# Loading Q, K and V in more, smaller DMAs: five opening loads and all loads of the regular groups are split in two

## The chip, the cores and the metric

The kernel runs on one core of one Trainium2 chip. The metric is device time in microseconds (us) of one execution, as the median of several runs. Engines are named as in the profile: PE is TensorE (PEld its weight loads), DVE is VectorE, ACT is ScalarE, POOL is GpSimd, SP is SyncE, which only issues DMAs here. A "q" behind a name (SPq) is the engine's sequencer.

## What is computed

A retention layer (attention with a decay in place of the softmax) feeds a bilinear feed-forward layer. Q, K and V are float32 of 8 batches x 8 heads x 576 positions x 64.

```python
scores = scale * np.matmul(q, k.transpose(0, 1, 3, 2))
gamma = 1.0 - 2.0 ** (-5.0 - np.arange(H))
Dmat = np.where(rel >= 0, gamma[:, None, None] ** rel, 0.0)
attn = np.matmul(scores * Dmat, v)              # rel = query position - key position
x = attn.transpose(0, 2, 1, 3).reshape(4608, 512)
out = ((x @ w_a) * (x @ w_b)) @ w_out           # 512 -> 1536 -> 512
```

## The kernel before

**Stages.** The 4608 rows of x are made in groups of 256 rows and taken by the feed-forward layer in blocks of 512, 256, 256 and then 512 rows. The feed-forward matmuls (lines 771, 794 and 809 for the two first products, 828 for the last) run through the whole kernel; the retention work of later groups is put between them at places written out by hand.

- *Opening and third batch, by steps.* The first 256 rows of batches 0, 1 and 2 are handled in six steps, `STEPS`, each a batch and four of its heads. `load_step` (line 155) loads four heads of Q, K or V of one step: partition p holds rows 2p and 2p + 1 of each head, so a run in memory is 512 bytes and a load is 256 KB. Twelve such loads (steps 0 to 3) open the kernel in an order written out by hand: step 0's Q, K, V; step 2's Q, K; step 1's K, Q; step 2's V; step 3's K, Q; step 1's V; step 3's V. All are issued by SP but step 0's K, which ACT issues. Steps 4 and 5 are loaded later in the same way.
- *Regular groups.* Groups 3 to 17 hold 256 rows each of all eight heads. `load_pair` (line 139) loads Q, K and V of one; each tensor in two DMAs, one for each 128 rows (all heads, runs of 256 bytes, 256 KB). Two of the groups (15 and 17) hold the last 64 rows of eight batches and are loaded in four DMAs of 64 rows (128 KB) for each tensor; they are called left-over groups.

**What uses the loads.** Of a step, `cast_step` (line 311) turns Q and K to bfloat16 on DVE, ACT or POOL, `values_step` (319 and 321) scales V by the decay, the transposes (329) run on PE and are copied by ACT or DVE (333), and the scores, states and outputs follow on PE. ACT also makes tables (213, 223) and copies states (386 to 391). Of a regular group, `ahead` casts Q and K on POOL, the first 64 partitions in one instruction (484) and the other 64 in two (488), and scales V (495); for groups 4 and 5 K and V are cast one half (128 rows) at a time. `turn` (507) then issues from SP two DMA transposes of the casts. `keyed` (538), `matched` (600), `from_states` (628) and `keys_into` (641) are the group's matmuls.

**Order.** Every engine works through its instructions in the order of the program. SP's order is: the opening loads; a tiny DMA `gate` (line 930) that waits for the first third of `w_out`; the loads of steps 4 and 5; group 3; group 4's Q; then in turn the transposes of one group, the loads of a later group, and stores of finished rows (lines 750 and 752). Places of this order are numbers in a list, `todo`, along the feed-forward work. Weights are loaded by POOL's own DMA queue (lines 264, 266 and 269), the first of them behind POOL's casts of the opening.

Of the kernel before, what the change touches and what calls it, by code (L numbers as in the profile page):

```python
# [18 lines left out]
def kernel(  # L19
# [10 lines left out]
    nc = tc.nc  # L30

    B, H, S, D = q.shape
    DM = H * D
# [30 lines left out]
    def rows_of(n):  # L64

        if n not in LEFT:
            b, m = PAIRS[n]
            return [(kp, 0, 128, b, 256 * m + 128 * kp) for kp in (0, 1)]
        return [(i // 2, 64 * (i % 2), 64, 4 * LEFT[n] + i, S - 64)
                for i in range(4)]  # L70
# [67 lines left out]
    paired = {}  # L138

    def load_pair(n, which=(0, 1, 2)):  # L140
        if n >= NP:
            return
        paired.setdefault(n, {})
        for i in which:
            name, src = (("qf", q), ("kf", k), ("vf", v))[i]
            t = stage.tile([128, 2 * DM], FP32, tag=name, name=name + "2")
            for kp, r0, m, b, s0 in rows_of(n):
                nc.sync.dma_start(
                    t[r0:r0 + m, kp * DM:(kp + 1) * DM]
                    .rearrange("p (h d) -> p h d", h=H),  # L150
                    src[b, :, s0:s0 + m, :].rearrange("h s d -> s h d"))
            paired[n][i] = t

    def load_step(n, hh, which, on=nc.sync):

        if n not in paired:
            paired[n] = [stage.tile([128, 2 * DM], FP32, tag=name, name=name)
                         for name in ("qf", "kf", "vf")]
        on.dma_start(  # L159
            paired[n][which][:, hh * DM:(hh + 1) * DM]  # L160
            .rearrange("p (h e) -> p h e", h=4),
            (q, k, v)[which][n, 4 * hh:4 * hh + 4, 0:256, :]
            .rearrange("h (p two) d -> p h (two d)", two=2))

    STEPS = [(0, 0), (1, 0), (0, 1), (1, 1), (2, 0), (2, 1)]
    Q, K, V = 0, 1, 2
    for i, which in ((0, Q), (0, K), (0, V), (2, Q), (2, K), (1, K),
                     (1, Q), (2, V), (3, K), (3, Q), (1, V), (3, V)):
        load_step(*STEPS[i], which,
                  nc.scalar if (i, which) == (0, K) else nc.sync)  # L170

# [327 lines left out]
    def turn(n):  # L501
        qkb = of(natural, n)[0]
        qkT = qkt_pool.tile([128, 2, 2, HP, 128], BF16, tag="qkT",
                            name="qkT2")
        transposed[FIRST + n, "pair"] = qkT
        for w in (Q, K):
            nc.sync.dma_start_transpose(
                qkT[:, w].rearrange("p k c s -> p (k c) s"), qkb[:, w])
        if n > 10:
            load_pair(n + 2)  # L510
# [420 lines left out]
    for i, which in ((4, Q), (4, K), (4, V), (5, Q), (5, K), (5, V)):  # L931
        load_step(*STEPS[i], which)
    load_pair(FIRST)
    load_pair(FIRST + 1, (Q,))


# [131 lines left out]
```

## Time and profile before

| | us |
|---|---|
| median of 3 runs (324.93 to 325.23) | 325.18 |
| the profiled execution | 325.43 |
| its span (first to last instruction) | 323.7 |

DMAs by kind in that execution, with the median time from issue to landing:

| DMA | number, size | us to landing |
|---|---|---|
| Q, SP | 32 of 256 KB, 8 of 128 KB | 4.7, 3.2 |
| K, SP | 31 of 256 KB, 8 of 128 KB | 4.8, 3.5 |
| V, SP | 32 of 256 KB, 8 of 128 KB | 5.2, 4.2 |
| K of step 0, ACT | 1 of 256 KB | 4.0 |
| transposes, SP | 30 | 3.7 |

"Issue" is the time that an instruction takes on the issuing engine, waits included; "to landing" counts from the start of the issue until the last part of the data has been reported as written. In a line of the timeline the columns are start and length in us, engine, line, operation, tile, shape, number of instructions and, in brackets, how long the engine had been idle and what ended it.

### The profile page before, as it was taken

The page shows a single profiled execution, that of the slowest core. Times are in us where ns is not written, and L with a number is a line of the kernel's source. Part 1 is how long each engine was busy: PE and PEld are TensorE (multiplying, and loading weights), DVE is VectorE, ACT ScalarE, POOL GpSimd, SP SyncE. Part 2 cuts the span into 40 slices and gives each one's busy share as a digit, 9 for nine tenths or more (in the row PEclk, how much of TensorE's full clock was granted, in tenths as well). Part 3 has the DMA queues.
Part 4 walks back from the last instruction along what each step waited for, and adds up shares of the span by engine and source line. Part 5 has one row for each costly group of instructions (what it writes and reads, how often), then busy time and mean ns, then how long its engine had stood idle before and what let it go on. Part 6 is the DMA issues. An engine that isn't in the chain of part 4 may idle for free.

```text
span 323.7 us, 8631 instructions
## 1 busy us (share of the span) xinstructions
PE 314.0 (97%) x3573; PEld 164.4 (51%) x3611; DVE 165.4 (51%) x294; ACT 131.5 (41%) x293; POOL 118.8 (37%) x158
## 2 busy tenths in 40 slices
PE   7899999999999999999999999999999999999996
PEld 3564457778444554444454545454445444444444
DVE  5744445665546754835374626562566256514321
ACT  7735753463435523533253324442433343313321
POOL 4990077574755274447165305450530000000000
PEclk9999999999999999999999999999999999999999
DMA  8999999999999999999999169935840520031013
GB/s 216 255 196 207 259 231 189 200 176 206 174 221 223 195 208 206 269 222 263 175 197 216 52 163 198 207 74 144 194 86 19 104 76 2 2 97 32 1 23 108
DMA packets 145431, 50.90 MB, mean 157 GB/s; under 512 B 126704, under 2 KB 140912, under 8 KB 145392
## 3 DMA queue, kind: packets, MB, share of 16 engines
q1 hardware_dynamic: 140112, 45.37, 68.4%
q0 software_dynamic: 4752, 4.72, 8.8%
q8 instruction: 28, 0.46, 0.6%
q10 hardware_dynamic: 528, 0.26, 0.3%
q14 instruction: 11, 0.09, 0.1%
HBM read 37.75 MB, written 9.44 MB: 146 GB/s over the span
## 4 chain that ended last, share of the span: by engine, by line
PE 92%; DMA 2%; SPq 2%; ACT 1%; issue 1%; DVE 1%; DVEq 0%
PE pb L809 29%; PE po L828 29%; PE pa L794 28%; DMA qf<-in_q_dram 2%; SPq L159 2%; PE sc L600 1%; PE o L628 1%; PE o L641 1%; PE kv L538 1%; PE pa L771 1%; ACT state_after L386 0%; ACT vb L319 0%; PE tp L329 0%; DVE hT L814 0%; ACT own L390 0%
## 5 line engine op out<-in xcount | busy, mean ns | idle before, releaser
L814 DVE TENSOR_TENSOR hT<-ha,pb 128x512 bf16<-128x512 bf16 (+1 forms) x120 | 75.9, 633 | 94.8 <-PE pb L809 86.6
L802 ACT CAST ha<-pa 128x512 bf16<-128x512 f32 (+1 forms) x120 | 64.8, 543 | 115.9 <-PE pa L794 109.9
L809 PE MATMUL pb<-xT,wb_sb 128*128 128x512 bf16 (+1 forms) x474 | 111.2, 357 | 0.5
L794 PE MATMUL pa<-xT,wa_sb 128*128 128x512 bf16 (+1 forms) x452 | 106.9, 356 | 1.2 <-issue 0.6
L828 PE MATMUL po<-wo_sb,hT 128*128 128x512 bf16 (+2 forms) x442 | 94.7, 367 | 1.7 <-issue 1.4
L809 PEld LDWEIGHTS <-wb_sb 128*128 128x128 bf16 x480 | 47.0, 98 | 46.6 <-issue 0.3
L794 PEld LDWEIGHTS <-wa_sb 128*128 128x128 bf16 x468 | 45.0, 98 | 44.4 <-issue 0.2
L828 PEld LDWEIGHTS <-hT 128*128 128x128 bf16 x456 | 42.7, 98 | 47.2
L484 POOL CAST qkb<-qf 64x1024 bf16<-64x1024 f32 x15 | 15.5, 1031 | 64.4 <-DMA qf<-in_q_dram 55.1
L495 POOL TENSOR_TENSOR vb<-vf,vs 128x1024 bf16<-128x1024 f32 (+1 forms) x17 | 28.9, 1700 | 13.3 <-DMA vf<-in_v_dram 6.1
L839 DVE COPY osb<-po 128x512 f32<-128x512 f32 (+2 forms) x17 | 11.1, 653 | 43.0 <-PE po L828 43.0
L837 ACT COPY osb<-po 128x512 f32<-128x512 f32 (+1 forms) x21 | 12.0, 573 | 43.4 <-PE po L828 40.5
L484 POOL CAST qkb<-kf 64x1024 bf16<-64x1024 f32 (+1 forms) x17 | 16.4, 966 | 16.7 <-DMA kf<-in_k_dram 16.5
L563 DVE TENSOR_TENSOR sums<-kv,sums 128x256 f32<-128x256 f32 x44 | 18.7, 424 | 2.8 <-PE kv L538 0.8
L609 DVE TENSOR_TENSOR sT<-sc,mask 128x512 bf16<-128x512 f32 x30 | 19.4, 681 | 0.0
L488 POOL CAST qkb<-kf 64x512 bf16<-64x512 f32 (+1 forms) x34 | 18.7, 579 | 1.0
L488 POOL CAST qkb<-qf 64x512 bf16<-64x512 f32 x30 | 17.6, 615 | 0.6
L567 ACT CAST states<-sums 64x512 bf16<-64x512 f32 x26 | 16.0, 617 | 0.3
L654 DVE TENSOR_TENSOR xT<-o,qs 128x512 bf16<-128x512 f32 x24 | 15.4, 682 | 1.5 <-PE o L641 1.5
L311 POOL CAST qkb<-kf 128x512 bf16<-128x512 f32 x5 | 3.1, 617 | 16.9 <-DMA kf<-in_k_dram 16.9
L355 DVE TENSOR_TENSOR sT<-sc,mask_s 128x1024 bf16<-128x1024 f32 x6 | 7.2, 1222 | 1.3 <-PE sc L347 1.2
L855 PE MATMUL w<-ones 128*128 128x512 bf16 x17 | 6.3, 482 | 1.5 <-DVE idxp_f L204 1.5
(88 smaller groups left out, 163.5 us busy)
## 6 DMA issues: line engine op xcount, KB each, us to landing
qf<-in_q_dram SPq DMA_DIRECT2D x32, 256.0 KB, 4.7
vf<-in_v_dram SPq DMA_DIRECT2D x32, 256.0 KB, 5.2
kf<-in_k_dram SPq DMA_DIRECT2D x31, 256.0 KB, 4.8
out_dram<-osb SPq DMA_DIRECT2D x25, 256.0 KB, 3.2
out_dram<-osb SPq DMA_DIRECT2D x21, 128.0 KB, 2.6
wo_sb<-in_moe_w_out_dram POOLq DMA_DIRECT2D x3, 512.0 KB, 16.7
qf<-in_q_dram SPq DMA_DIRECT2D x8, 128.0 KB, 3.2
kf<-in_k_dram SPq DMA_DIRECT2D x8, 128.0 KB, 3.5
```

What stands on the lines that cost most here:

```text
L484: nc.gpsimd.tensor_copy(qkb[0:64, w, e], t[0:64, e])
L488: nc.gpsimd.tensor_copy(to[:, :, 1 - r], fro[:, :, r])
L495: nc.gpsimd.tensor_tensor(vb[:, e].rearrange("p (h d) -> p h d", d=D), t[:, e].rearrange("p (h d) -> p h d", d=D), decay[:, at], op=ALU.mult)
L563: nc.vector.tensor_tensor(sums[:, i], own, prev, op=ALU.add)
L567: nc.scalar.copy(to(half(1 - r)), fro(half(r)))
L609: nc.vector.tensor_tensor(sT[:, on].rearrange("p c k s -> p (c k) s"), sc[:, on].rearrange("p c k s -> p (c k) s"), mask3.unsqueeze(1).to_ ...
L654: nc.vector.tensor_tensor(x_of(t0, 128).rearrange("p c (a s) -> p c a s", a=2), o[:, :, :, kp].rearrange("p a c s -> p c a s"), qs[:, :, s ...
L794: nc.tensor.matmul(pa[:, 0:n], wa_sb[:, c, fs], xT[:, c], start=(c == 0), stop=(c == NC - 1))
L802: nc.scalar.copy(ha[:, 0:n], pa[:, 0:n])
L809: nc.tensor.matmul(pb[:, 0:n], wb_sb[:, c, fs], xT[:, c], start=(c == 0), stop=(c == NC - 1))
L814: nc.vector.tensor_tensor(hT[:, F, 0:n], has[F][:, 0:n], pb[:, 0:n], op=ALU.mult)
L828: nc.tensor.matmul(po[:, 0:width], hT[:, F, u * 128:(u + 1) * 128], wo_sb[:, F, cols], start=(F == 0), stop=(F == NF - 1))
```

## The change

In `load_pair`, a DMA for 128 rows becomes two: heads 0 to 3, then heads 4 to 7 (128 KB each). The 64-row DMAs of the left-over groups stay whole. In `load_step` a new argument `parts` says into how many DMAs of equal numbers of heads a load goes; the opening list gives 2 to five loads (step 2's Q and K, step 1's Q, step 3's K, step 1's V) and 1 to the seven others. The loads of steps 4 and 5 use the default, 1. The order of the loads, the bytes, the tiles and all instructions that read them stay.

```diff
-                nc.sync.dma_start(
-                    t[r0:r0 + m, kp * DM:(kp + 1) * DM]
-                    .rearrange("p (h d) -> p h d", h=H),
-                    src[b, :, s0:s0 + m, :].rearrange("h s d -> s h d"))
+                heads = H if m < 128 else H // 2
+                for h in range(0, H, heads):
+                    e0 = kp * DM + h * D
+                    nc.sync.dma_start(
+                        t[r0:r0 + m, e0:e0 + heads * D]
+                        .rearrange("p (h d) -> p h d", h=heads),
+                        src[b, h:h + heads, s0:s0 + m, :]
+                        .rearrange("h s d -> s h d"))
...
-    def load_step(n, hh, which, on=nc.sync):
+    def load_step(n, hh, which, on=nc.sync, parts=1):
...
-        on.dma_start(
-            paired[n][which][:, hh * DM:(hh + 1) * DM]
-            .rearrange("p (h e) -> p h e", h=4),
-            (q, k, v)[which][n, 4 * hh:4 * hh + 4, 0:256, :]
-            .rearrange("h (p two) d -> p h (two d)", two=2))
+        for h in range(0, 4, 4 // parts):
+            hs = slice(4 * hh + h, 4 * hh + h + 4 // parts)
+            on.dma_start(
+                paired[n][which][:, 128 * hs.start:128 * hs.stop]
+                .rearrange("p (h e) -> p h e", h=4 // parts),
+                (q, k, v)[which][n, hs, 0:256, :]
+                .rearrange("h (p two) d -> p h (two d)", two=2))
...
-    for i, which in ((0, Q), (0, K), (0, V), (2, Q), (2, K), (1, K),
-                     (1, Q), (2, V), (3, K), (3, Q), (1, V), (3, V)):
+    for i, which, parts in ((0, Q, 1), (0, K, 1), (0, V, 1), (2, Q, 2),
+                            (2, K, 2), (1, K, 1), (1, Q, 2), (2, V, 1),
+                            (3, K, 2), (3, Q, 1), (1, V, 2), (3, V, 1)):
```

More of the change, by code (lines that the diff above doesn't have):

```diff
@@ L158, in load_step @@
                          for name in ("qf", "kf", "vf")]
-        on.dma_start(
-            paired[n][which][:, hh * DM:(hh + 1) * DM]
-            .rearrange("p (h e) -> p h e", h=4),
-            (q, k, v)[which][n, 4 * hh:4 * hh + 4, 0:256, :]
-            .rearrange("h (p two) d -> p h (two d)", two=2))
+        for h in range(0, 4, 4 // parts):
[5 more added lines that the diff above has]
+                .rearrange("h (p two) d -> p h (two d)", two=2))
     STEPS = [(0, 0), (1, 0), (0, 1), (1, 1), (2, 0), (2, 1)]
     Q, K, V = 0, 1, 2
-    for i, which in ((0, Q), (0, K), (0, V), (2, Q), (2, K), (1, K),
-                     (1, Q), (2, V), (3, K), (3, Q), (1, V), (3, V)):
+    for i, which, parts in ((0, Q, 1), (0, K, 1), (0, V, 1), (2, Q, 2),
+                            (2, K, 2), (1, K, 1), (1, Q, 2), (2, V, 1),
+                            (3, K, 2), (3, Q, 1), (1, V, 2), (3, V, 1)):
         load_step(*STEPS[i], which,
-                  nc.scalar if (i, which) == (0, K) else nc.sync)
+                  nc.scalar if (i, which) == (0, K) else nc.sync, parts)
     idxp_i = const.tile([128, 2], INT32)
```

## The prediction

> **What bounds the kernel now.** I read the page's shares first, then the chain of work that ended last.
>
> ```profile
> span 323.7 us, 8631 instructions
> PE 314.0 (97%) x3573; PEld 164.4 (51%) x3611; DVE 165.4 (51%) x294; ACT 131.5 (41%) x293; POOL 118.8 (37%) x158
> ...
> PE 92%; DMA 2%; SPq 2%; ACT 1%; issue 1%; DVE 1%; DVEq 0%
> ```
>
> TensorE (PE) is busy for 314.0 of 323.7 us and is 92% of the chain. The rest, DMA, SP's issues and ScalarE (ACT), lies at the start. The second view is that chain in order of time, from 4 to 17 us (start, length, what).
>
> ```profile
> 6.56 5.51 DMA qf<-in_q_dram
> 12.07 0.02 issue
> 12.09 0.62 ACT qkb L311
> ...
> 14.09 0.95 ACT vb L319 x4
> ...
> 16.64 0.18 ACT second L391
> 16.82 0.27 PE pa L771
> ```
>
> A Q load lands at 12.07 (step 3's, the tenth opening load), ACT casts it and is then busy link after link until 16.82, when the first feed-forward product may start. From 16.82 on the chain is TensorE to the end; the idle times that the groups show before its matmuls (0.5, 1.2 and 1.7 us for the three feed-forward lines) are over the whole run. So loads can be worth something in two ways only: a gain before 16.82, or a loss where TensorE comes to wait for a later load. The third view is the timeline of the opening, for the slack of that chain.
>
> ```profile
> 11.27 0.60 ACT L223 ACTIVATE qs_o<-qs_o,biasq,lgp 128x256 f32<-128x256 f32 x1
> 12.09 0.62 ACT L311 CAST qkb<-qf 128x512 bf16<-128x512 f32 x1 [0.22 <-DMA qf<-in_q_dram]
> ...
> 16.80 2.52 PEld L771 LDWEIGHTS <-wa_sb 128*128 128x128 bf16 x24 [0.17 <-DMA wa_sb<-in_moe_w_a_dram]
> ```
>
> ACT stood idle for 0.22 us before that cast. An earlier Q therefore gives 0.22 us at most, unless ACT's earlier work moves too; a later Q costs its whole delay.
>
> **The change, part by part.** It adds DMAs and removes none of the bytes. Five opening loads become ten DMAs. Thirteen regular groups (15 groups less the two of left-over rows) have three loads of two DMAs each, so 78 DMAs become 156. Together 83 more issues, all on SP.
>
> *Price of a half's issue.* No row shows a regular half (4 heads x 128 rows x 256 B). The nearest are the whole opening loads, 4 heads x 128 rows with runs of 512 B, at 0.45 to 0.51 us while SP is not held up, and the left-over loads, also 128 KB in runs of 256 B, but 8 heads x 64 rows, at 0.63 us. A whole regular load takes 0.57 to 0.63 us after a pause and 1.14 us when SP runs ahead of the transfers. I take 0.51 plus 0.04 between issues, 0.55 us, because the heads and rows are the same; the other end is 0.67. SP's timeline:
>
> ```profile
> 53.34 1.27 SPq L148 DMA_DIRECT2D kf<-in_k_dram  x2
> 54.72 1.90 SPq L148 DMA_DIRECT2D vf<-in_v_dram  x2
> 56.79 4.56 SPq L507 DMA_TRANSPOSE qkT<-qkb  x2
> ...
> 64.74 3.77 SPq L148 DMA_DIRECT2D vf<-in_v_dram  x2
> ...
> 190.56 2.78 SPq L148 DMA_DIRECT2D qf<-in_q_dram  x4
> ```
>
> Where SP runs ahead, two halves (1.10 us) cost no more than one whole (1.14 + 0.04), so groups 3 and 5 to 14 keep their pace: 78 x 0.55 = 43 us more of issuing is covered by SP's waiting for the transfers. If a half costs 0.67, twelve halves take 8.0 us where group 5's six wholes took 7.05 (61.45 to 68.50): 1.0 us late at its end.
>
> *Where that cover is thin.* Group 4's K and V are issued at 53.34 onto a nearly drained queue, so wholes are cheap there: 53.34 to 56.62, against 8 x 0.55 = 4.4, to 57.7. Behind them on SP stand the transposes of group 4, which wait for the casts on POOL (GpSimd), and behind those group 5's loads.
>
> ```profile
> 56.99 0.61 POOL L484 CAST qkb<-kf 64x512 bf16<-64x512 f32 x1 [1.10 <-DMA kf<-in_k_dram]
> ...
> 58.45 0.61 POOL L484 CAST qkb<-kf 64x512 bf16<-64x512 f32 x1
> ...
> 59.94 1.04 POOL L495 TENSOR_TENSOR vb<-vf,vs 128x512 bf16<-128x512 f32 x1
> ...
> 64.31 0.45 PE L600 MATMUL sc<-qkT 64*64 64x64 bf16 x32
> ```
>
> The first cast wants all 8 heads of the first 128 rows, which now come with the second half, issued at 53.89. At 3.1 us to landing (smallest of the left-over loads) it is there at 56.99, as before; at the 3.6 us of the whole it is 0.55 late. The K transpose was issued at 59.88 and took 3.7 us: landed at 63.6, 0.7 us ahead of the matmul at 64.31. I take 0.1 us late, since two halves hold the bytes of one whole and the queue is nearly empty; it is hidden. The same slack is 1.6 us at group 3 (52.0 + 3.6 against 57.16), 1.9 at group 5 (71.9 + 3.1 against 76.93) and more than 2 at the later groups. Middle: 0, bounds 0 and +0.65 (below, as a rival). A gain is excluded, because TensorE waits for no load there.
>
> *More landings to wait for.* A consumer of a split tile waits for two to four landings. Such semaphore waits show as 17 ns on SP; 15 POOL instructions in the tight stretch would add some 0.2 us at most, inside the 0.7.
>
> *The opening.* SP's first loads (step 0's Q and V) are unchanged, K is on ACT. Then come Q2 and K2 in halves, K1, Q1 in halves, V2, K3 in halves, Q3, V1 in halves, V3. At 0.55 each Q3 would be issued at 0.80 + 11 x 0.55 = 6.9, against 6.56. The trace's records give the DMAs eight completion semaphores in turn, and a DMA waits for the landing of the one eight places before it: Q3 then waits for K2's first half, shortly before 7.57 (K2's landing, 2.40 + 5.2), and goes at about 7.3. Before, it took 5.5 us from issue to landing in a queue that was never empty: the transfers are behind, not SP. About 4.7 us of time are left to 12.07 and the left-over loads need 3.1 to 4.5, so Q3 lands where the queue brings it. Value 0. Bounds: -0.22 (the idle time of ACT) and +0.1 from the semaphore waits.
>
> The rate of the transfers gives the reason for the lower bound (stretch, its length, busy times of PE, PEld, DVE, ACT, POOL, clock, DMA share, GB/s):
>
> ```profile
> 3.00:4.50 1.50, 1.50 (x5) 0.45 (x3) 0.36 (x2) 1.45 (x7) 0.07 (x1) 1.00 1.15 343
> 5.00:12.00 7.00, 5.90 (x130) 3.54 (x133) 4.97 (x9) 5.19 (x14) 4.28 (x7) 1.00 1.17 290
> 61.50:64.50 3.00, 2.95 (x100) 1.82 (x101) 1.80 (x4) 1.90 (x5) 1.04 (x1) 1.00 1.15 256
> 65.00:68.00 3.00, 2.84 (x19) 1.37 (x15) 2.83 (x7) 1.90 (x4) 1.65 (x3) 1.00 1.23 220
> ```
>
> Each time the rate is higher before SP's issues stretch and lower once they are stretched. If halves keep SP from running ahead, the fast rate may last.
>
> A rule speaks against the change: "DMA: Bandwidth & Descriptors" of the Trainium skill, Rules for kernel authors, wants many small transfers joined into large ones, and its Anatomy of one DMA gives a fixed cost of about 2.0 us each (for the software path). Paid one after another, 83 of them would be 166 us, and the estimate 491 us. The trace disagrees with paying them in series: loads take 4.0 to 5.6 us to land and yet leave SP every 0.5 to 1.1 us.
>
> **Sum.** 0 + 0. The profiled execution took 325.43 us (span 323.7 and 1.7 around it), 0.25 over the median of 325.18; so about 325.2 us.
>
> **Rivals.**
> *The weights get in front of V (slower).* The first weight load leaves POOL at 9.07 and lands 7.7 us later; step 3's V was issued at 8.53 and lands 5.4 later, at 13.9, and ACT's scaling by it is on the chain at 14.09. With halves V goes out at about 9.1, level with the weights. From the moment that it falls behind them it waits for their transfer: 384 KB at some 200 GB/s, 2.0 us, less the 0.16 of slack: up to +1.8, 327.0; when they mix, half of it, 326.1. For it: the tiny gate DMA needed 5.2 us behind weights. Against it: V's issue still begins no later. The same page (Queues, rings and completion order) says that the engines take turns between queues packet by packet; by that V would be delayed in part, while the gate's 5.2 us looks more like first come, first served, which spares V.
>
> *Group 4 is late (slower).* With issues every 0.67 us the sixth half (V's first rows) goes at 56.69 and lands 4.6 later (as V did there), at 61.3, 1.35 us after POOL wanted it at 59.94; less 0.7 of slack, TensorE waits 0.65 us: 325.8. The point is a delay of 0.7. For it: the smallest slack of all. Against it: the halves need less time to land.
>
> *The fast rate lasts (faster).* 7.5 us at 290 GB/s would be 6.3 at 343: Q3 1.17 us earlier. ACT takes 0.22 of it, 325.0, within no change; if its work before moves as well, all of it, 324.0. Against: a V load of step 0, which is not split, feeds ACT first, and TensorE's order sits between.
>
> **How the numbers follow.** A measurement of this kernel can tell about 0.2%, 0.65 us. No change, 0.45 with the small gain in it. Weights in front of V, 0.2; group 4 or a slower transfer of halves in other groups, 0.18: together slower 0.38. Faster 0.17. The likeliest gives 325.2. Its own range is 324.9 to 325.8; the rivals stretch it to 324.2 and 326.9.
>
> **What would show it.** Right: Q3's landing still near 12.1, the first feed-forward product at 16.6 to 16.9, the matmul of group 4 at 64.3 with no wait, SP's halves at about 0.55 us. Wrong: the rate after 5 us near 343, V after 14.1, or TensorE waiting at a line of the groups (538, 600, 628).

## The result, and the profile after

| | before | after |
|---|---|---|
| median of the runs taken side by side (22 each), us | 325.19 | 326.27 |
| lowest and highest, us | 324.90, 327.49 | 325.31, 328.41 |
| after / before (95%) | | 1.0032 (1.0019 to 1.0045) |
| the profiled execution, us | 325.43 | 325.31 |
| its span, us | 323.7 | 323.6 |

The change makes the kernel 0.32% slower, 1.1 us. The executions of the new kernel also spread more: 6 of its 22 lie between 325.3 and 325.7, the 16 others from 326.05 upwards. Of the kernel before, 20 of 22 lie below 326. The profiled execution of the new kernel is its quickest, so its page can show where the change makes the kernel tighter, but hardly the loss. The slowest, 328.41, is no measure of the change: it ran at a mean granted clock of 0.995 in place of 1.000, and so did one execution of the kernel before beside a later run (327.94; more in the last section). All line numbers are 7 higher than before.

The page of the new kernel, head, first line of part 1 and the chain that ended last:

```profile
span 323.6 us, 8794 instructions
...
PE 317.5 (98%) x3611; PEld 164.1 (51%) x3611; DVE 165.6 (51%) x294; ACT 131.3 (41%) x293; POOL 117.9 (36%) x158
...
PE 94%; DMA 3%; POOL 1%; DVE 1%; issue 0%; SPq 0%; DVEq 0%; POOLq 0%
```

TensorE is the whole bound, as before. (3573 matmuls were recorded before and 3611 now, the same number as weight loads: 38 records were missing then.) The opening, by ACT's timeline and by the windows that the prediction used:

```profile
12.15 0.62 ACT L318 CAST qkb<-qf 128x512 bf16<-128x512 f32 x1 [0.20 <-DMA qf<-in_q_dram]
...
14.03 1.07 ACT L326 ACTIVATE vb<-vf,vs 128x64 bf16<-128x64 f32 x4
```

```profile
3.00:4.50 1.50, 1.50 (x5) 0.45 (x3) 0.33 (x2) 1.44 (x7) 0.06 (x1) 1.00 1.15 342
5.00:12.00 7.00, 6.28 (x132) 3.48 (x133) 4.92 (x9) 5.21 (x14) 4.21 (x7) 1.00 1.18 290
61.50:64.50 3.00, 3.00 (x132) 1.85 (x131) 1.70 (x5) 1.62 (x4) 1.51 (x2) 1.00 0.94 194
65.00:68.00 3.00, 3.00 (x16) 1.35 (x15) 2.93 (x7) 2.19 (x4) 0.03 (x1) 1.00 0.80 178
```

Step 3's Q is there at 12.13 (before 12.07) and the idle time in front of its cast is 0.20 (before 0.22). The rate after 5 us is 290 GB/s in both kernels. In the same two stretches of the regular groups it fell, from 256 and 220 GB/s to 194 and 178, and the DMA engines are no longer always busy: 128 KB every 0.55 us are 238 GB/s at most, and SP begins group 5's loads later. SP's timeline shows it, first at groups 4 and 5:

```profile
53.38 2.21 SPq L151 DMA_DIRECT2D kf<-in_k_dram  x4
55.70 2.09 SPq L151 DMA_DIRECT2D vf<-in_v_dram  x4
57.97 4.03 SPq L514 DMA_TRANSPOSE qkT<-qkb  x2
62.10 2.21 SPq L151 DMA_DIRECT2D qf<-in_q_dram  x4
64.35 3.15 SPq L151 DMA_DIRECT2D kf<-in_k_dram  x4
67.60 2.10 SPq L151 DMA_DIRECT2D vf<-in_v_dram  x4
70.24 4.15 SPq L514 DMA_TRANSPOSE qkT<-qkb  x2
```

Four halves take 2.1 to 2.2 us, 0.55 each, as costed, but for those of 3.15, of which one alone took 1.49 us. Group 4's K and V were issued from 53.34 to 56.62 before and to 57.79 now. Group 4's transposes therefore begin at 57.97 in place of 56.79 and group 5's loads at 62.10 in place of 61.45. Their issuing ends at 69.70 in place of 68.50. The lateness is handed on: the transposes of groups 3 to 12 all begin 1.2 to 3.7 us later than before, and only those of group 13, ahead of which SP has time to spare in both kernels, begin on time again. Group 11's transposes before and after:

```profile
154.08 3.67 SPq L507 DMA_TRANSPOSE qkT<-qkb  x2
```

```profile
157.01 2.85 SPq L514 DMA_TRANSPOSE qkT<-qkb  x2
```

SP begins them 2.9 us later, and K's, the second of the two, 1.9 later. The product that wants them, on TensorE's timeline before and after:

```profile
162.94 0.50 PE L600 MATMUL sc<-qkT 64*64 64x64 bf16 x32
```

```profile
162.59 0.50 PE L607 MATMUL sc<-qkT 64*64 64x64 bf16 x32
```

Their K lands at 162.33, 0.26 us ahead of it; before it landed at 159.66, 3.3 us ahead. So this execution has no wait, but its margins are nearly used up. Worked out from the landings in the trace, this is the time from the landing of a group's K transpose to its product `sc` (line 600 before, 607 after), in us:

| group | 3 | 4 | 5 | 6 | 8 | 9 | 10 | 11 | 13 | 14 |
|---|---|---|---|---|---|---|---|---|---|---|
| before | 1.6 | 0.7 | 1.9 | 6.8 | 6.5 | 4.8 | 5.9 | 3.3 | 4.3 | 7.4 |
| after | 1.7 | 0.1 | 0.4 | 5.8 | 3.7 | 2.0 | 2.1 | 0.3 | 4.3 | 7.5 |

In this execution, a landing that comes half a microsecond later would make TensorE wait at group 4, 5 or 11, and would have cost nothing before.

Not all of this is SP's doing. The products themselves come 0.3 us earlier than before, because the opening ended 0.3 earlier: of the 0.6 us that group 4 lost, only 0.34 are a later landing. And at group 5 the K loads landed at 69.67, no later than before (69.76). What was late there was Q: one sixteenth of its last part came 1.31 us behind the fifteen others, so POOL began its casts at 67.97 in place of 66.31, and K's transpose, which waits for them, went out 1.25 later. At groups 8 to 11 no such accident is needed, as two more profiles of this kernel below show.

### The profile page after: what moved, and what is told of

It is laid out like the page before. It is cut to its first block, busy times and chain, and to the rows that moved or that the text cites. A ratio compares the mean times of both kernels' runs of the same rounds, so it can differ in the third digit from the quotient of the medians.

```text
span 323.6 us, 8794 instructions
## 1 busy us (share of the span) xinstructions
PE 317.5 (98%) x3611; PEld 164.1 (51%) x3611; DVE 165.6 (51%) x294; ACT 131.3 (41%) x293; POOL 117.9 (36%) x158
## 4 chain that ended last, share of the span: by engine, by line
PE 94%; DMA 3%; POOL 1%; DVE 1%; issue 0%; SPq 0%; DVEq 0%; POOLq 0%
PE po L835 29%; PE pb L816 29%; PE pa L801 28%; DMA vf<-in_v_dram 3%; PE o L635 1%; PE sc L607 1%; PE o L648 1%; PE kv L545 1%; PE pa L778 1%; POOL vb L328 1%; PE o L444 0%; PE tp L336 0%; DVE hT L821 0%; POOL wb_sb L273 0%; PE kv L381 0%
## 5 line engine op out<-in xcount | busy, mean ns | idle before, releaser
L801 PE MATMUL pa<-xT,wa_sb 128*128 128x512 bf16 (+1 forms) x468 | 108.9, 357 | 0.0
L835 PE MATMUL po<-wo_sb,hT 128*128 128x512 bf16 (+2 forms) x456 | 97.0, 368 | 0.0
```

Of the source, the lines that this page charges most:

```text
L801: nc.tensor.matmul(pa[:, 0:n], wa_sb[:, c, fs], xT[:, c], start=(c == 0), stop=(c == NC - 1))
L835: nc.tensor.matmul(po[:, 0:width], hT[:, F, u * 128:(u + 1) * 128], wo_sb[:, F, cols], start=(F == 0), stop=(F == NF - 1))
```

## The experiments

The times are medians, with the lowest and highest and the number of runs. Every ratio is to the kernel before, run on the same chip, with its 95% interval. All edits are to the changed kernel unless something else is said.

### The opening alone, the regular groups alone

```diff
-                heads = H if m < 128 else H // 2
+                heads = H
```

> Only the five opening loads are split; the regular groups load whole. Theory A (the loss is TensorE waiting at groups 3 to 5, whose data come with under 2 us to spare): same as before, 324.8 to 325.4 us. Theory B (the opening is late: split loads or weights in front of V): about +1.0, 326.2 us, first feed-forward product after 17.3. Theory C (every added DMA costs a little anywhere): 5 of 83, +0.07, 325.3 us.

Measured: 325.53 us (325.13 to 326.09, 12), ratio 1.0008 (1.0000 to 1.0016).

The other part alone keeps line 148 and gives the opening's list the number 1 everywhere:

```diff
-    for i, which, parts in ((0, Q, 1), (0, K, 1), (0, V, 1), (2, Q, 2),
-                            (2, K, 2), (1, K, 1), (1, Q, 2), (2, V, 1),
-                            (3, K, 2), (3, Q, 1), (1, V, 2), (3, V, 1)):
+    for i, which, parts in ((0, Q, 1), (0, K, 1), (0, V, 1), (2, Q, 1),
+                            (2, K, 1), (1, K, 1), (1, Q, 1), (2, V, 1),
+                            (3, K, 1), (3, Q, 1), (1, V, 1), (3, V, 1)):
```

> Opening loads whole, all regular groups in halves. Theory A: the whole loss, 325.9 to 326.6 us. Theory B: same as before, 325.2 us. Theory C: 78 of 83, 326.2 us.

Measured: 326.64 us (325.12 to 327.29, 12), ratio 1.0032 (1.0017 to 1.0046). The regular groups alone have the whole loss and the whole spread: 4 executions at 325.1 to 325.8, 8 at 326.3 to 327.3. The four quick ones are the first four on record and the eight others follow, so something may have changed between them that the record does not show; the profile, 325.78, is of the first. The opening's halves cost 0.3 us at the median, at the edge of what can be told from no loss.

### Which groups

Opening whole in the first, third and fourth, halves only in the groups named:

```diff
-                heads = H if m < 128 else H // 2
+                heads = H if m < 128 or n not in (3, 4, 5) else H // 2
```

> Halves only in groups 3, 4 and 5 (18 of the 83 added DMAs). Theory A: nearly the whole loss, 325.8 to 326.5 us. Theory B: same, 325.2 us. Theory C: +0.23, 325.4 us.

Measured: 326.00 us (325.52 to 326.76, 12), ratio 1.0018 (1.0002 to 1.0033).

The reverse, with the opening split as in the change:

```diff
+                heads = H if m < 128 or n in (3, 4, 5) else H // 2
```

> As the changed kernel, but groups 3, 4 and 5 load whole. Theory A: within 0.3 us of before, 325.0 to 325.5 us. Theory B: the whole loss, 326.2 us. Theory C: 65 of 83, +0.84, 326.0 us.

Measured: 325.74 us (325.44 to 326.58, 12), ratio 1.0019 (1.0011 to 1.0028).

```diff
+                heads = H if m < 128 or n not in (9, 10, 11) else H // 2
```

> Halves only in groups 9, 10 and 11 (18 added DMAs), all else as before. Theory A: some of the loss, 325.3 to 325.7 us, by margins that fall from 3 to 6 us to 0.3 to 2 in the changed kernel's trace. Theory C: +0.23, 325.4 us. With the next run: A wants more here than there, C 18 to 42.

Measured: 325.88 us (325.40 to 326.70, 11), ratio 1.0014 (1.0003 to 1.0026).

```diff
+                heads = H if m < 128 or 3 <= n <= 5 or 9 <= n <= 11 else H // 2
```

> Halves only in groups 6, 7, 8, 12, 13, 14 and 16 (42 added DMAs), whose margins stay above 3 us. Theory A: same as before, 325.0 to 325.4 us. Theory C: +0.54, 325.7 us.

Measured: 325.94 us (325.44 to 328.52, 13), ratio 1.0015 (1.0004 to 1.0025).

No part of the groups carries the loss alone. The three parts, 0.18, 0.14 and 0.15%, add up to 0.47, and together they cost 0.32; the intervals allow both. Theory A (TensorE waits at the groups with small margins) missed three times: the groups with large margins were to cost nothing, groups 9 to 11 more than those, and without groups 3 to 5 the time was to stay within 325.5. Theory C (a fixed price for each added DMA) fits no better: 18 DMAs cost as much as 42. Three of the four intervals nearly reach zero. These four runs spread the loss over the kernel; they do not divide it.

### Later products, to give the margins back

Two stretches of the list of places are moved 4 and 8 places later. They hold the steps with the products of groups 4 and 5 and of later groups, but also the casts, transposes, stores and loads that have their places there (the loads of groups 7 and 8 among them), so more was moved than the expectation says. The same is done to the kernel before, as a control.

```diff
+    todo = [(at + sum(d for lo, hi, d in ((190, 270, 4), (450, 650, 8)) if lo <= at < hi), fn, args)
+            for at, fn, args in todo]
     todo.sort(key=lambda e: e[0])
```

> The changed kernel with TensorE's places of groups 4 and 5 four units later (about 0.9 us) and those of groups 9 to 11 eight units later (1.7 us); the loads do not move. Theory A (late data at the groups with the least margin): most of the loss goes, 325.2 to 325.6 us. Theory C (a price for each added DMA, wherever it is): no help, 326.2 us or more.

> The kernel before with the same later places, as the control: both theories 324.9 to 325.4 us; anything above is the price of the move itself (later products for the next block), to be taken off the run beside it.

Measured: 329.83 us (4 runs), ratio 1.0128 (1.0107 to 1.0149), for the changed kernel; 330.39 us (5 runs), ratio 1.0139 (1.0117 to 1.0162), for the kernel before. The move itself costs 5 us, which was not expected. The timeline of TensorE in the control, and the end of the chain that led to the first of its two waits:

```profile
72.09 0.60 PE L794 MATMUL pa<-xT,wa_sb 128*128 128x256 bf16 x4 [1.58 <-ACT ha L802]
...
87.17 0.21 PE L628 MATMUL o<-qkT,states 64*64 64x64 bf16 x1 [1.79 <-ACT states L567]
```

```profile
71.36 0.40 ACT left_states L567
71.77 0.28 ACT ha L802
72.04 0.04 issue
72.09 0.60 PE pa L794 x4
```

ACT copies states first and the feed-forward layer's `ha` behind them, and TensorE waits for both, 1.58 and 1.79 us. Behind the second wait the granted clock is 0.50 for 3.41 us, which takes 1.7 more; three of the control's five executions have such a stretch (mean clock 0.995), one of the changed kernel's four. These losses hide the one sought: with the moved steps the changed kernel is not slower than the control, and its margins at groups 4, 5 and 11 are 1.9, 3.6 and 3.3 us, but waits of other kinds have been put in. Inconclusive.

### More issues on SP, larger and smaller transfers

The kernel before, with one more DMA behind each of its 78 regular loads. It brings 8 bytes into a tile that nothing reads, so the transfers stay whole and SP alone gets more to do.

```diff
+    tiny = []
+    tinies = const.tile([1, 160], FP32, name="tinies")
...
             t[r0:r0 + m, kp * DM:(kp + 1) * DM]
             .rearrange("p (h d) -> p h d", h=H),
             src[b, :, s0:s0 + m, :].rearrange("h s d -> s h d"))
+                if m == 128:
+                    e = 2 * len(tiny)
+                    tiny.append(e)
+                    nc.sync.dma_start(tinies[:, e:e + 2],
+                                      src[b, 0, s0:s0 + 1, 0:2])
```

> As before, with a tiny DMA (8 bytes into a tile that nothing reads) on SP behind each of the 78 whole regular DMAs: the same number of issues as in the changed kernel, but whole transfers. If SP's issue time and place in the order make the loss: 325.8 to 326.6 us. If the smaller transfers make it (their landing or their rate): 325.0 to 325.4 us.

Measured: 325.92 us (325.24 to 326.88, 12), ratio 1.0019 (1.0006 to 1.0031); the profiled execution took 326.42. Here the loss can be seen. SP's timeline, then TensorE's:

```profile
63.32 0.38 SPq L150 DMA_DIRECT2D qf<-in_q_dram  x1
63.74 0.43 SPq L157 DMA_DIRECT2D tinies<-in_q_dram  x1
64.21 0.38 SPq L150 DMA_DIRECT2D kf<-in_k_dram  x1
64.63 0.43 SPq L157 DMA_DIRECT2D tinies<-in_k_dram  x1
...
71.12 4.14 SPq L514 DMA_TRANSPOSE qkT<-qkb  x2
```

```profile
77.17 0.45 PE L607 MATMUL sc<-qkT 64*64 64x64 bf16 x32 [0.32 <-DMA qkT<-qkb]
...
163.87 0.45 PE L607 MATMUL sc<-qkT 64*64 64x64 bf16 x32 [0.27 <-DMA qkT<-qkb]
```

Eight bytes take 0.43 us of SP, a half of 128 KB 0.51. The transposes of group 5 start at 71.12, later than in either kernel, and TensorE stands idle in front of `sc` of groups 5 and 11. Read as the lag of TensorE's weight loads against the kernel before, the waits cost 0.50 us at group 5, about 0.1 at group 8 and 0.45 at group 11. From the first feed-forward product to the end this execution takes 308.24 us, the kernel before 306.91: +1.33 us, of which these waits make 1.0. So more issuing on SP is enough for a loss of this kind and size, without any smaller transfer. At the median it cost 0.19% against 0.32 for the regular halves; the intervals overlap, so a part of the halves' loss may have another cause.

The other way, quarters: opening whole, regular loads of 128 rows in four DMAs of two heads.

```diff
-                heads = H if m < 128 else H // 2
+                heads = H if m < 128 else H // 4
```

> Opening whole; every regular load of 128 rows in four DMAs of two heads (234 more issues than before). Theory A (SP's issues push the data of the next groups back, until TensorE waits): 24 issues of about 0.55 us a group are 13 us, and with transposes and stores SP fills the 17 us that TensorE takes for a group; margins at groups 4 and 5 of 0.7 and 1.9 us are overrun by several us, TensorE waits there and at 9 to 11: 330 to 345 us, and the matmuls of the groups show the waits. Theory C (a fixed price for each added DMA, 1.07 us / 83): 328.2 us with no wait at the groups.

Measured: 383.99 us (382.71 to 385.95, 4 runs), ratio 1.1807 (1.1772 to 1.1842), far beyond every number expected (theory A had 330 to 345 us with waits at the groups' products, theory C 328.2 with none). The chain on its page, and lines of its list of waits (total, times, longest):

```profile
PE 56%; SPq 28%; DMA 6%; issue 4%; ACT 2%; POOL 1%; DVE 1%; POOLq 0%; DVEq 0%
```

```profile
PEld L607 <- DMA qkT<-qkb: 32.3, 8, 7.6
PE sc L607 <- DMA qkT<-qkb: 31.4, 8, 7.5
...
PE kv L545 <- POOL vb L502: 10.9, 5, 6.2
```

SP's timeline of it, and TensorE's:

```profile
48.39 4.48 SPq L151 DMA_DIRECT2D vf<-in_v_dram  x8
52.98 4.00 SPq L151 DMA_DIRECT2D qf<-in_q_dram  x8
57.07 3.39 SPq L514 DMA_TRANSPOSE qkT<-qkb  x2
```

```profile
62.46 0.64 PE L607 MATMUL sc<-qkT 64*64 64x64 bf16 x32 [5.04 <-DMA qkT<-qkb]
...
74.86 0.45 PE L607 MATMUL sc<-qkT 64*64 64x64 bf16 x32 [2.75 <-DMA qkT<-qkb]
```

A quarter costs 0.47 us of SP and 0.04 between issues, little less than a half. Group 3's transposes start at 57.07 (before 48.75), and TensorE waits 31.4 us in eight groups for K transposes: the same row as with the tiny DMAs, 50 times as long. SP has no time left over and makes 28% of the chain. That refutes a fixed price for each DMA. On top of it comes the granted clock, 0.50 in or behind every wait of 2.7 us or more (last section).

### The changed kernel again

> The changed kernel once more, for a second profile: an execution near its median, 326.3 us. Theory A: TensorE waits at the matmuls of groups 4, 5 or 9 to 11. Other theories: at the start, or spread evenly.

Measured: 325.50 us, not near the median but again one of the quick executions, with margins of 1.1, 2.4 and 1.3 us at groups 4, 5 and 11 and no wait there.

> The changed kernel once more, for a profile of one of its slower executions (most of its timed executions took 326 us or more, while both profiled so far were among its fastest). SP's order (A): if this execution takes 326 us or more, the waits are at the products sc of groups 4, 5, 8, 9, 10 or 11, 0.1 to 0.6 us each, together 0.5 to 1.5 us, with the K transposes landing after TensorE asks; nothing is lost at groups 13 and 14. Opening (B): the loss lies before 17 us, with the first feed-forward product after 17.0, and no group's product waits. If it takes under 325.7 us, it says nothing new and both stay.

Measured: 326.42 us (before beside it 324.96). No product of a group waits. The loss lies before 17.5 us, so on this execution the theory of the opening (B) was right and that of SP's order (A) was not. Its chain that ended last, and TensorE's timeline:

```profile
9.03 6.05 DMA vf<-in_v_dram
15.10 1.07 ACT vb L326 x4
...
17.49 2.77 PE pa L778 x24
```

```profile
15.50 0.97 PE L381 MATMUL kv<-vb,qkb 64*64 64x64 bf16 x16 [0.73 <-ACT vb L326]
```

Step 3's V lands at 15.08, against 13.92 in the quick execution, and the first feed-forward product comes at 17.48 (16.51). After it the two take the same: 307.22 and 307.09 us. The trace reports a landing in sixteen parts, one by each DMA engine. The last four parts of that V (us):

```
after, profiled first      13.71  13.73  13.83  13.92
after_third                13.80  13.85  13.93  15.08
```

One engine is 1.15 us behind the fifteen others. In the packet records an instruction DMA (16 KB of program, the queue "instruction" of the page) begins at 12.71 in this execution and takes 1.16 us. The records do not name its engine, but time and length fit. In the quick executions it begins at 12.82 and 12.87, V is on time, and a part of the weights behind V is late, by 0.9 to 1.2 us. The changed kernel with later products had it at 12.47, and V at 14.91; with the opening's halves alone it began at 12.79, and V was on time. So this lateness comes or stays away by a tenth of a microsecond.

The same lateness sets the first product in most of the quick openings, split or whole. The first load of `w_a` is complete when its last sixteenth lands, 0.8 to 1.3 us behind the others, and TensorE's first feed-forward weight load starts 0.04 to 0.05 us later in eight of the fourteen profiles:

| | last part of `w_a` | first weight load |
|---|---|---|
| before (opening whole) | 16.76 | 16.80 |
| regular_halves (whole) | 16.75 | 16.79 |
| halves_3_to_5 (whole) | 16.40 | 16.44 |
| whole_plus_tiny (whole) | 16.43 | 16.47 |
| after (split) | 16.46 | 16.51 |
| after_again (split) | 16.42 | 16.46 |
| opening_halves (split) | 16.34 | 16.39 |

(The eighth is the control with later products, 16.79 and 16.83.) So the 0.3 us by which the first product comes earlier in the changed kernel's profile is not the work of the halves.

The margins in the profiles of `after_again` and `after_third` (us, to be read with the table of the first profile):

| group | 3 | 4 | 5 | 6 | 8 | 9 | 10 | 11 | 13 | 14 |
|---|---|---|---|---|---|---|---|---|---|---|
| after_again | 2.0 | 1.1 | 2.4 | 6.8 | 4.0 | 2.0 | 2.9 | 1.3 | 4.3 | 7.5 |
| after_third | 2.2 | 1.0 | 1.2 | 6.1 | 3.2 | 1.4 | 1.6 | 0.4 | 4.3 | 7.5 |

At groups 8 to 11 all three profiles have 2 to 4 us less than before, and the profile of the regular halves alone agrees (2.4, 1.2, 2.2 and 1.2). At groups 4 and 5 it is not so regular: two of the three have more at group 4 than before, one has more at group 5.

The three profiles and the tiny DMAs side by side (us):

| | execution | first product | from there to the end |
|---|---|---|---|
| before | 325.43 | 16.81 | 306.91 |
| after | 325.31 | 16.51 | 307.09 |
| after_again | 325.50 | 16.46 | 307.33 |
| after_third | 326.42 | 17.48 | 307.22 |
| whole_plus_tiny | 326.42 | 16.47 | 308.24 |

Two ways of losing one microsecond are thus shown: a late V in the opening (in the changed kernel), and waits at the products of the groups (with tiny DMAs and with quarters, but in no profile of the changed kernel or of the regular halves). How often each happens in the changed kernel, and so what makes its median, stays open. That the opening is not the greater part rests on two runs: with the opening's halves alone no execution of 12 reached 326.1, and with the regular halves alone 8 of 12 passed 326.2 with an opening written as before. This is no proof, since an opening can be late with whole loads too: in the profile of halves_elsewhere the first product came at 17.94 (last section).

## Why the prediction was right or wrong

*Opening, 0 (bounds -0.22 and +0.1): right as the usual case, but not by its reason.* Q3 was expected near 12.1 and landed at 12.13. It left SP at 7.40: the sum counts 11 issues ahead of it, and there are 12, which gives 7.4 without the wait for K2 that was put in to reach 7.3. The first product was expected at 16.6 to 16.9 and came at 16.51. The step took ACT's chain, which ends at 16.82, for what lets the first product start. In the changed kernel ACT's last link ends at 16.87, 0.36 after that product began: what released it is the landing of `w_a`, as the table above shows, and a line of the prediction's own third view says so for the kernel before (`L771`, idle time of 0.17 us ended by the DMA of `wa_sb`). An earlier Q alone could not have brought the first product forward in these executions. The halves alone measured +0.08%, below the 0.2% set for no change.

*The fast rate lasts: did not happen.* The rate after 5 us is 290 GB/s in both kernels.

*Weights in front of V: not as written, but its price was real.* V lands at 13.8 to 13.9 in two profiles of the changed kernel, at 15.1 in the third, and at 14.9 with the later products. What holds it is, by its time and length, not the weight queue but an instruction DMA on one of the sixteen engines; the loss is 1.0 us where the rival had 0.9 to 1.8, and that the two agree is luck. The prediction had no step for such a DMA, although the page of before lists 28 of them.

*Price of a half, 0.55: right.* 0.51 us and 0.04 between issues.

*Group 4, 0.1 late against a slack of 0.7: 0.34 late in the first profile, and not by the term that was costed.* The cast that the step watched was not late, on POOL's timeline after:

```profile
56.79 0.61 POOL L491 CAST qkb<-kf 64x512 bf16<-64x512 f32 x1 [1.71 <-DMA kf<-in_k_dram]
```

It ran at 56.99 before. But the step itself had V's last issue end at 57.7 (measured 57.79) and did not carry that on to the transposes that stand behind it on SP: they begin 1.2 us later, K's was issued 0.87 later and landed 0.34 later, and with the product 0.3 earlier the slack falls from 0.7 to 0.1. In the two other profiles it is 1.0 and 1.1. The rival "group 4 is late" had the right kind of wait, a product without its K; but no profile with halves shows it at group 4, and the tiny DMAs show it at groups 5 and 11. What the extra landings to wait for cost POOL, nothing in these profiles tells apart.

*"Groups 3 and 5 to 14 keep their pace: 78 x 0.55 = 43 us more of issuing is covered by SP's waiting for the transfers": this is the step that failed.* It compared two halves with one whole at the places where SP runs ahead, and took the pause as free. Group 5's twelve halves took 7.60 us where six wholes took 7.05, and they started 0.65 late. What SP loses it hands on, because everything of it is in one order: transposes, loads, stores. By group 11 the transposes are 2.9 us later. The slacks of "more than 2 at the later groups" were not checked against a lateness that is handed on: group 11's 3.3 became 0.3, 1.3 and 0.4 in the three profiles. That this lateness then makes TensorE wait is shown with more issues of another kind (1.0 us with the tiny DMAs, 31.4 with the quarters); in the changed kernel itself no such wait was caught, so how much of its 1.1 us is due to this step stays open.

*The second half of the same error:* the slacks were read from one execution and used to the last tenth. Landings vary by 1 us and more (in the trace of before single sixteenths of loads come up to 1.6 us behind the others). A slack of 0.3 to 0.4 us is then no cover. The forecast was made from a quick execution and met another within 0.1 us (325.2 against 325.31); the median is made by the others. The measured 326.27 lies outside the range that the likeliest case had for itself, 324.9 to 325.8, and in the wide one, 324.2 to 326.9, only because two rivals stretched that; neither happened as it was written. That the wide range holds it is luck. No change had 0.45; the sign fell on the side that had 0.38.

*The rule to join small transfers* (the Trainium skill, "DMA: Bandwidth & Descriptors", Rules for kernel authors) pointed the right way. Its price of about 2.0 us for each DMA, paid in series, did not hold: 83 more DMAs cost 1.1 us. The same page (Issuing engines are not separate DMA queues) calls the sequencer's time to start a DMA usually small beside the DMA itself. The trace agrees for one, 0.55 against 3.2 to 3.5 us to landing. The sum is another matter: with 156 regular loads in one order the margins at groups 8 to 11 shrank, and with 312 (the quarters) SP was 28% of the chain.

## What to carry to other kernels

- An engine that only issues DMAs has a budget too. Count its issues by a measured price (here 0.4 to 0.6 us, whether 8 bytes or 256 KB) over the period of a loop, and look at what stands behind them in its order; a lateness that is not caught up by a pause is handed to the next round.
- Where a wait does not exist, write down its margin at every place of the loop, before and after, and compare it with the spread of the landings, not with zero.
- If most executions of a kernel are slower than the one profiled, profile it again: a quick execution shows the margins, not the loss, and even margins differ by a microsecond from one execution to the next.

## What the runs showed of the hardware

*Instruction DMAs.* Every execution has 28 of them, on the page of the new kernel:

```profile
q8 instruction: 28, 0.46, 0.6%
```

0.6% of sixteen engines' span is about 1.1 us of one engine for each (0.006 x 16 x 323.6 / 28); the records say 0.9 to 1.7, mostly near 1.05. Loads that are then in flight have one sixteenth late: in the trace of before such a DMA runs from 66.33 to 67.31, and of group 5's two K loads fifteen parts had landed by 67.40 and 68.56 and the last came at 68.97 and 69.76.

TensorE may also wait for such a DMA itself. In the opening it stands still in front of one and the same matmul, the eighth of sixteen of a product `o`, with no releaser in the profile, and goes on 1.3 to 1.6 us after the first instruction DMA has ended:

| | first instruction DMA, from and to | idle | goes on at |
|---|---|---|---|
| after_again | 12.82, 13.96 | 0.22 | 15.43 |
| before | 13.20, 14.37 | 0.25 | 15.70 |
| halves_9_to_11 | 13.34, 14.35 | 0.30 | 15.87 |
| halves_elsewhere | 14.48, 15.37 | 0.93 | 16.93 |

This fits a wait for the program's next piece. No semaphore shows it, so it is not proved.

*The clock after a short wait.* The profiled execution of halves_elsewhere, at 328.52 us its slowest, has its opening loads whole, and V is on time (13.86). TensorE was idle for 0.93 us in the opening, at the place just described, and then ran at a granted clock of 0.50 for 3.41 us. Its timeline of TensorE, and its windows:

```profile
16.93 0.32 PE L444 MATMUL o<-sT,vb 64*64 64x128 bf16 x9 [0.93 <-issue]
```

```profile
14.00:16.00 2.00, 1.65 (x72) 1.23 (x72) 1.88 (x3) 1.99 (x8) 2.00 (x4) 1.00 1.32 204
16.00:17.70 1.70, 0.77 (x27) 0.53 (x26) 0.57 (x2) 1.30 (x7) 1.70 (x3) 1.00 1.24 170
17.70:21.10 3.40, 3.40 (x27) 2.47 (x18) 1.18 (x2) 0.00 (x0) 3.20 (x9) 0.50 1.22 202
```

At half the clock for 3.4 us, TensorE does 1.7 us less work; with the idle time that is the 2.6 us by which this execution lies above its median. The other executions with a mean clock of 0.995, 328.41 of the changed kernel and 327.94 of the kernel before, were not profiled, but the same stretch would give that mean (1.7 of 327 us).

In the kernel with quarters all seven stretches at 0.50 begin a whole number of 3.41 us from one another (62.12, 75.77, 116.73, 140.62, 161.10, 188.41, 212.30) and last one, two or three times 3.41. So the clock seems to be set anew at fixed times 3.41 us apart and not a certain time behind a wait: the first stretch begins at 62.12, within the wait of 5.04 us that ends at 62.46, and the second at 75.77, 0.9 us behind the end of the wait of 2.75. A wait of 1.19 us there (until 90.88), and waits of half a microsecond at a group's product (whole_plus_tiny), brought no such drop. In halves_elsewhere TensorE was busy for 63% of the 3.41 us ahead of the drop.
